# Attention and two feed-forward layers on one core: later chunks of the weights kept as 32-bit words until block 1, and a later place for block 2's attention

## The chip, the cores and the metric

The kernel runs on one core of a Trainium2 chip. The metric is device microseconds of a whole execution. Several executions were timed and their median counts; one more was recorded by the hardware profiler, and the trace comes from it. TensorE is the matrix engine, DVE the vector engine, ACT the scalar engine, POOL the general one, and SP issues every DMA of this kernel.

## The reference

The inputs q, k and v are float32 of 4 batches, 8 heads, 576 positions and 64 elements. The weights of the feed-forward layers are float64.

```
scores = q k^T / 8                       # per batch and head
keep the 32 largest of each row; softmax over these
x = attn v, heads side by side           # 2304 tokens x 512
h = relu(x w_in);  x = (h*h) w_out       # w_in 512x2048, w_out 2048x512
h = max(x w1, x w2, x w3);  out = h w_out2   # w1..w3 512x768, w_out2 768x512
```

## The kernel before

**Blocks.** The 2304 tokens are worked on in six blocks of 384 columns. The list `units` says which 128-row tiles of which batch belong to a block. Block 0 is three tiles of batch 0; block 1 is the rest of batch 0 and the first tile of batch 1; block 2 is the other three tiles of batch 1, and blocks 3 to 5 do the same for batches 2 and 3. For each block, `attend` runs four times (one pair of heads each), and then `moe` runs both feed-forward layers. Block 2 finds the keys and values of batch 1 prepared already, and loads queries only; the calls of block 3 load and prepare those of batch 2.

**Attention.** A job is one head of one tile, 24 jobs or more to a block. TensorE makes the scores (L525), ACT writes them to `s` (L446), DVE takes the 32 largest in four rounds of max8 and match_replace (L452, L454), ACT forms the exponentials (L312, L460), ACT and POOL split them into two f16 halves (L463, L309), SP transposes both by DMA (L468), TensorE multiplies by the values (L479), POOL divides and adds (L530 to L538), and TensorE transposes into the feed-forward operand `xt`, which ACT and DVE write as a high and a low part (L507, L509; L491, L493 for the 64 remaining rows). All four pairs of a block must be there before its first feed-forward matmul.

**Weights.** A weight is used as a pair: a rounded part and the remainder. Its source is float64, so it is converted once. There are 28 chunks of two halves, 16 for the first layer, 9 for w1 to w3 and 3 for w_out2. `half_chunk` converts a half: it loads 512 KB of raw float64 into one of three slots (L588), ACT makes a float from the high words (L589, recorded at L312) and takes the missing low bits from bytes (L592), DVE joins both into an exact 32-bit word in a buffer `ot` (L594, 3 buffers; the list `joined` keeps these operations), ACT rounds it (L597), POOL subtracts (L598, recorded at L309), and SP stores the 512 KB pair to DRAM (L599). The first 18 chunks (`EARLY`) are converted during block 0's attention, two halves to a job. The other ten are converted in block 0's feed-forward just ahead of their use, straight into one of seven `wt` buffers, and stored from there. Every later block loads pairs from DRAM to `wt` (L576).

**Order.** Nothing is left to run-time choice. `Plan` writes down one order for each engine at build time: a list scheduler takes, among what is ready on an engine, what can start first, by estimated times and with a small weight for priority. `fix_order` then holds each engine to it. Buffers of a tag are opened in the order of the program. `plan.after` adds a soft dependence: an operation may not start, in the plan's estimate, before the named one starts. It sets no semaphore. For the pairs of blocks 2 to 5 (`i >= NP * 3`) it names `joined[-9]`, the ninth last of the 56 joins, for everything that `attend` issues, the loads too; `moe` is free of it.

Of the kernel before, what the change touches and what calls it, by code (L numbers as in the profile page):

```python
# [10 lines left out]
F32 = mybir.dt.float32  # L11
F32R = mybir.dt.float32r
# [9 lines left out]
P = 128  # L22
# [227 lines left out]
def c_act(n, psum=True, ptr=0):  # L250
    return (55.0 if psum else 95.0) + 0.834 * n + 93.0 * ptr
# [6 lines left out]
def c_pool(n):  # L258
    return 100.0 + 2.18 * n
# [7 lines left out]
def kernel(ctx, tc, q, k, v, w_in, w_out, w1, w2, w3, w_out2, out):  # L267
    nc = tc.nc
# [3 lines left out]
    NP = H // 2  # L272
# [11 lines left out]
    dr = ctx.enter_context(tc.tile_pool(name="dr", bufs=1, space=DRAM))  # L284
    plan = Plan(nbufs, {"b"})

    def buf(tag, shape, dtype=F32):
        return Buf(plan, ppool if tag in ("a", "b") else spool, shape, dtype, tag)

    def keep(tile_):  # L290
        return Buf(plan, None, None, None, None, fixed=tile_)

    def act(prio, n, reads, writes, fn, psum=True, ptr=0):
        plan.op(ACT, c_act(n, psum, ptr), prio, reads, writes, fn)

    def dve(prio, n, reads, writes, fn, rate=1.0, slack=0.0):
        return plan.op(DVE, c_dve(n, rate), prio, reads, writes, fn, slack=slack)

    def gps(prio, n, reads, writes, fn):
        plan.op(POOL, c_pool(n), prio, reads, writes, fn)  # L300
# [4 lines left out]
    def dma(prio, nbytes, reads, writes, fn, ns=650.0):  # L305
        plan.op(SP, ns, prio, reads, writes, fn, lat=max(nbytes / DBW, 90.0))

    def sub(eng, out_ap, a, b):
        eng.tensor_tensor(out_ap, a, b, op=ALU.subtract)  # L309

    def prelu(out_ap, src, slope, **kw):
        return nc.scalar.activation(out_ap, src, AF.Prelu, alpha=slope, **kw)  # L312


    C_D, C_A, C_P, C_M = 1, 0, 0, 1
    A_S, A_X, A_E, A_V, M_, W_, MA, MP, MD = 0, 1, 2, 2, 4, -1, -1, 0, 0
# [25 lines left out]
    EARLY, PER = 18, 2  # L342
# [75 lines left out]
    def attend(i, unit, p):  # L418
# [18 lines left out]
        for j, h in jobs:  # L437
            for _ in range(min(PER if g == 0 else 0, len(ahead))):
                half_chunk(False, *ahead.pop(0))
# [104 lines left out]
    joined = []  # L544
# [8 lines left out]
    for fp in range(NF2):  # L553
        chunk_src.append(w_out2[fp * 256:(fp + 1) * 256, :].rearrange("(k p) f -> p k f", p=P))
    NCH = len(chunk_src)
    scratch = [[keep(dr.tile([P, 1024], F32, name=f"wsc{n}_{x}")) for x in range(2)] for n in range(NCH)]

    def weights(g, n):

        src = chunk_src[n]  # L560
        a, f = src.shape[1], src.shape[2]
        h = a // 2
        wts = [half_chunk(g > 0 or n < EARLY, n, x) for x in range(2)]

        def view(r, kk):
            return wts[kk // h][:, r].rearrange("p (a f) -> p a f", f=f // 2)[:, kk % h]
        return (lambda kk: wts[kk // h]), view

    def half_chunk(again, n, x):

        src = chunk_src[n]
        h, f = src.shape[1] // 2, src.shape[2]
        src = src[:, x * h:(x + 1) * h, :]
        wt, dst = buf("wt" if again or n >= EARLY else "cw", [P, 2, 512], F32R), scratch[n][x]
        if again:
            dma(W_, P * 4096, [dst], [wt], lambda: nc.sync.dma_start(  # L576
                wt[:].rearrange("p a b -> p (a b)").bitcast(F32), dst[:]))
            return wt
        raw = work[(2 * n + x) % len(work)]
        cv = buf("ot", [P, 512])  # L580

        def bits(t=U32):
            return spare[:].rearrange("p x a b -> p (x a b)")[:, 1024 * raw[1]:1024 * raw[1] + 1024].bitcast(t)

        def word(u):
            return bits().rearrange("p (n u) -> p n u", u=2)[:, :, u]

        dma(W_, P * 4096, [], [raw], lambda: nc.sync.dma_start(bits().rearrange("p (a f) -> p a f", f=f), src))  # L588
        act(C_M, 512, [raw], [cv], lambda: prelu(  # L589
            cv[:], word(1).bitcast(F32), -2.0 ** 32, scale=2.0 ** -112), psum=False)  # L590
        lw = buf("lw", [P, 512], U32)
        act(C_M, 512, [raw], [lw], lambda: nc.scalar.activation(  # L592
            lw[:], bits(U8).rearrange("p (n u) -> p n u", u=8)[:, :, 3], AF.Copy, scale=1.0 / 32.0, bias=-15.5 / 32.0), psum=False)
        joined.append(dve(C_D, 512, [cv, lw], [cv], lambda: nc.vector.scalar_tensor_tensor(  # L594
            cv[:].bitcast(U32), cv[:].bitcast(U32), 3, lw[:], op0=ALU.logical_shift_left, op1=ALU.bitwise_or),
            rate=1.7, slack=SL / 2))
        act(C_A, 512, [cv], [(wt, 0)], lambda: nc.scalar.copy(wt[:, 0], cv[:]), psum=False)  # L597
        gps(C_P, 512, [cv, (wt, 0)], [(wt, 1)], lambda: sub(nc.gpsimd, wt[:, 1], cv[:], wt[:, 0].bitcast(F32)))  # L598
        dma(W_, P * 4096, [wt], [dst], lambda: nc.sync.dma_start(  # L599
            dst[:], wt[:].rearrange("p a b -> p (a b)").bitcast(F32)))  # L600
        return wt

    def moe(g):
# [14 lines left out]
        def nextw():  # L618
            w = weights(g, cn[0])
            cn[0] += 1  # L620
            return w
# [94 lines left out]

    ahead = [(n, x) for n in range(EARLY) for x in range(2)]
    for i in range(NP * len(units)):
        plan.after = joined[-9] if i >= NP * 3 else None
        u = units[i // NP]  # L720
        attend(i, u, i % NP)
        if i % NP == NP - 1 and (i // NP == len(units) - 1 or units[i // NP + 1][3] != u[3]):
            plan.after = None
            moe(u[3])
# [66 lines left out]
```

## Time and profile before

| | |
|---|---|
| median of 3 runs | 1076.9 us (1076.82 to 1080.04) |
| profiled execution | 1079.8 us, span in the trace 1078.0 us |
| TensorE matmul busy | 984.3 us (91%) |
| TensorE weight load busy | 889.7 us (83%) |
| DVE busy | 818.7 us (76%) |
| ACT busy | 767.8 us (71%) |
| POOL busy | 625.3 us (58%) |
| mean granted TensorE clock | 0.958 |

Busy shares of the whole span hide the stages: attention and conversion run in the first part, and the last part has feed-forward layers alone. In the rows below, a `windows` row gives the stretch, and for each engine its busy time and, in brackets, its instructions; a timeline row gives start, duration, engine, line, operation, output and inputs, how many were merged, and in square brackets how long the engine sat idle before it and what released it. SPq is SP's queue, which issues DMAs in order and can wait.

### The profile page before, as it was taken

How to read it: one execution, taken by the hardware profiler on the slowest of the kernel's cores; microseconds unless marked ns; L12 is line 12 of the kernel's file. 1: busy time of each engine (PE TensorE's matmuls, PEld its weight loads, DVE VectorE, ACT ScalarE, POOL GpSimd, SP SyncE). 2: the span in 40 equal slices, each digit the busy share in tenths (PEclk: the TensorE clock that was granted, in tenths of full speed). 3: DMA queues.
4: the chain of work that ended last, by engine and by line, in shares of the span. 5: the costliest groups of instructions: out<-in, count | busy, mean ns of one | idle time of the engine just before them, and what ended most of it. 6: DMA issues, size and time to landing. Idle time of an engine off the chain costs nothing.

```text
span 1078.0 us, 18812 instructions
## 1 busy us (share of the span) xinstructions
PE 984.3 (91%) x6116; PEld 889.7 (83%) x6116; DVE 818.7 (76%) x1736; ACT 767.8 (71%) x1616; POOL 625.3 (58%) x887
## 2 busy tenths in 40 slices
PE   5556576999998999999999999999999999999998
PEld 3333343799897899998999998999998999989997
DVE  5999899899976999999999999999999601100020
ACT  6987788899887889976788868888876742123311
POOL 2666677787787577756467676767565641112210
PEclk9999755799999999999999999999999999999999
DMA  9999899999998999999999999999999986787774
GB/s 306 348 308 251 256 285 332 245 269 231 251 341 318 316 348 283 288 288 256 300 261 266 281 284 274 267 237 262 254 256 280 285 261 237 252 266 262 257 239 147
DMA packets 249697, 295.04 MB, mean 274 GB/s; under 512 B 178944, under 2 KB 182528, under 8 KB 249600
## 3 DMA queue, kind: packets, MB, share of 16 engines
q1 hardware_dynamic: 249600, 293.85, 95.1%
q8 instruction: 48, 0.79, 0.3%
q14 instruction: 49, 0.40, 0.1%
HBM read 217.25 MB, written 34.08 MB: 233 GB/s over the span
## 4 chain that ended last, share of the span: by engine, by line
PE 61%; DVE 13%; ACT 11%; POOL 7%; DMA 4%; issue 3%; SPq 0%; POOLq 0%; ACTq 0%; DVEq 0%
PE a L630 37%; PE b L630 13%; DVE mx L452 7%; DVE w L454 6%; PE b L525 5%; PE b L479 4%; DMA xt<-in_moe_w_in_dram 2%; POOL e L309 2%; ACT s L446 1%; ACT e L312 1%; POOL hl L309 1%; DMA xt<-in_moe_w_dram 1%; ACT lw L592 1%; ACT e L460 1%; ACT ot L312 1%
## 5 line engine op out<-in xcount | busy, mean ns | idle before, releaser
L452 DVE MAX8 mx<-w 128x8 f32<-128x576 f32 x432 | 311.1, 746 | 0.1
L309 POOL TENSOR_TENSOR e<-e,e 128x512 f16<-128x512 f32 (+1 forms) x288 | 211.9, 748 | 108.6 <-ACT e L463 91.3
L630 PE MATMUL a<-xt,wt 128*128 128x384 f32 x1296 | 239.3, 339 | 1.0 <-DVE xt L309 0.9
L630 PE MATMUL b<-xt,wt 128*128 128x384 f32 x1152 | 235.9, 346 | 3.5 <-DMA wt<-wsc 1.9
L630 PE MATMUL a<-hh,wt 128*128 128x384 f32 x768 | 228.8, 346 | 0.0
L630 PEld LDWEIGHTS a<-xt,wt 128*128 128x128 f32 x1296 | 224.1, 188 | 2.2 <-DVE xt L309 1.9
L454 DVE MATCH_REPLACE8 w<-mx,w 128x576 f32<-128x576 f32 x288 | 213.1, 742 | 0.0
L630 PEld LDWEIGHTS b<-xt,wt 128*128 128x128 f32 x1152 | 203.8, 192 | 5.8 <-DMA wt<-wsc 1.9
L525 PE MATMUL b<-kt,qt 128*128 128x288 f32 (+1 forms) x640 | 167.9, 395 | 36.2 <-DMA qt<-in_q_dram 17.8
L309 POOL TENSOR_TENSOR hl<-r,hh 128x384 fp32r<-128x384 f32 x96 | 97.3, 1014 | 126.5 <-ACT hh L656 119.2
L525 PEld LDWEIGHTS b<-kt,qt 128*128 128x128 f32 (+1 forms) x640 | 118.1, 218 | 62.5 <-ACT xs L482 16.4
L630 PEld LDWEIGHTS a<-hh,wt 128*128 128x128 f32 x768 | 142.7, 190 | 2.1 <-issue 1.1
L630 PE MATMUL a<-hl,wt 128*128 128x384 f32 x384 | 131.3, 342 | 4.1 <-POOL hl L309 3.8
L312 ACT ACTIVATE e<-s,mx 128x576 f32<-128x576 f32 x144 | 112.2, 779 | 27.7 <-POOL e L309 16.5
L479 PEld LDWEIGHTS <-et 128*128 128x128 f16 (+1 forms) x1440 | 84.1, 108 | 57.6 <-issue 35.4
L446 ACT ACTIVATE s<-b 128x288 f32<-128x288 f32 x288 | 108.0, 409 | 24.8 <-PE b L525 23.2
L479 PE MATMUL b<-vt,et 128*128 128x129 f16 (+3 forms) x1440 | 101.7, 223 | 25.2 <-DMA et<-e 16.8
L460 ACT ACTIVATE e<-e,nb 128x576 f32<-128x576 f32 x144 | 112.1, 779 | 6.8 <-POOL nb L456 4.8
L452 DVE MAX8 mx<-s 128x8 f32<-128x576 f32 x144 | 107.2, 746 | 10.3 <-ACT s L446 10.3
L454 DVE MATCH_REPLACE8 w<-mx,s 128x576 f32<-128x576 f32 x144 | 106.8, 742 | 0.0
L654 ACT ACTIVATE r<-b 128x384 f32<-128x384 f32 x96 | 47.1, 490 | 79.2 <-PE b L630 76.6
L463 ACT CAST e<-e 128x576 f16<-128x576 f32 x144 | 96.6, 672 | 1.6 <-DMA et<-e 1.3
(62 smaller groups left out, 1194.8 us busy)
## 6 DMA issues: line engine op xcount, KB each, us to landing
wt<-wsc SPq DMA_DIRECT2D x316, 512.0 KB, 4.8
wsc<-cw SPq DMA_DIRECT2D x36, 512.0 KB, 4.9
xt<-in_moe_w_out_dram SPq DMA_DIRECT2D x22, 512.0 KB, 6.3
wsc<-wt SPq DMA_DIRECT2D x20, 512.0 KB, 5.7
xt<-in_moe_w_dram SPq DMA_DIRECT2D x18, 512.0 KB, 5.9
xt<-in_moe_w_in_dram SPq DMA_DIRECT2D x16, 512.0 KB, 5.8
ks<-in_k_dram SPq DMA_DIRECT2D x12, 576.0 KB, 5.9
vst<-in_v_dram SPq DMA_DIRECT2D x16, 320.0 KB, 5.8
```

What stands on the lines that cost most here:

```text
L309: eng.tensor_tensor(out_ap, a, b, op=ALU.subtract)
L312: return nc.scalar.activation(out_ap, src, AF.Prelu, alpha=slope, **kw)
L446: act(A_S, HS, [ps], [(s, f)], lambda s=s, cs=cs, ps=ps: nc.scalar.activation(s[:, cs], ps[:, 0:HS], AF.Copy, scale=escale))
L452: dve(A_X, S, [src], [(mx, r)], lambda src=src, mx=mx, m8=m8: nc.vector.max(out=mx[:, m8], in_=src[:]))
L454: dve(A_X, S + 50, [src, (mx, r)], [w_], lambda src=src, mx=mx, m8=m8, w_=w_: nc.vector.match_replace(out=w_[:], in_to_replace=mx[:, m8], ...
L460: act(A_E, S, [e, nb], [e], lambda nb=nb, e=e: nc.scalar.activation(e[:], e[:], AF.Exp, bias=nb[:], scale=-1.0 / KEEP), psum=False, ptr=1)
L463: act(A_E, S, [e], [(e16, 0)], lambda e=e, e16=e16: nc.scalar.copy(e16[:, S:2 * S], e[:]), psum=False)
L479: nc.tensor.matmul(ps[0:m, 0:wv], et[:, mm_, c0:c1], vt[:, hh, vc, 0:wv], start=x == 0, stop=x == 8)
L525: nc.tensor.matmul(ps[:, 0:HS], a, c, start=m == 0, stop=m == len(seq) - 1)
L592: act(C_M, 512, [raw], [lw], lambda: nc.scalar.activation(lw[:], bits(U8).rearrange("p (n u) -> p n u", u=8)[:, :, 3], AF.Copy, scale=1.0 ...
L630: nc.tensor.matmul(o, x, y, start=first and i == 0 and m == 0, stop=last and i == n - 1 and m == 2)
L654: act(MA, N, [ps], [r], lambda r=r, ps=ps: nc.scalar.activation(r[:, 0:N], ps[:, 0:N], AF.Relu))
```

## The change

The ten chunks that are not converted early (20 halves) are stored by block 0 as joined 32-bit words, 256 KB a half, from `ot`. Block 0's own use of them stays as it was. Block 1 no longer loads pairs for these chunks: it loads the words into an `ot` buffer, rounds on ACT and subtracts on POOL into `wt`, and stores the pair of 512 KB to the place from which blocks 2 to 5 load it. The soft dependence of blocks 2 to 5's attention names the fifth last join in place of the ninth last.

```diff
+    words = [[keep(dr.tile([P, 512], F32, name=f"w32_{n}_{x}")) for x in range(2)] for n in range(NCH)]
...
-        wts = [half_chunk(g > 0 or n < EARLY, n, x) for x in range(2)]
+        wts = [split(n, x) if g == 1 and n >= EARLY else half_chunk(g > 0 or n < EARLY, n, x) for x in range(2)]
...
         act(C_A, 512, [cv], [(wt, 0)], lambda: nc.scalar.copy(wt[:, 0], cv[:]), psum=False)
         gps(C_P, 512, [cv, (wt, 0)], [(wt, 1)], lambda: sub(nc.gpsimd, wt[:, 1], cv[:], wt[:, 0].bitcast(F32)))
+        if n >= EARLY:
+            dma(W_, P * 2048, [cv], [words[n][x]], lambda: nc.sync.dma_start(words[n][x][:], cv[:]))
+            return wt
         dma(W_, P * 4096, [wt], [dst], lambda: nc.sync.dma_start(
             dst[:], wt[:].rearrange("p a b -> p (a b)").bitcast(F32)))
         return wt
 
+    def split(n, x):
+
+        wt, dst, cv = buf("wt", [P, 2, 512], F32R), scratch[n][x], buf("ot", [P, 512])
+        dma(W_, P * 2048, [words[n][x]], [cv], lambda: nc.sync.dma_start(cv[:], words[n][x][:]))
+        act(C_A, 512, [cv], [(wt, 0)], lambda: nc.scalar.copy(wt[:, 0], cv[:]), psum=False)
+        gps(C_P, 512, [cv, (wt, 0)], [(wt, 1)], lambda: sub(nc.gpsimd, wt[:, 1], cv[:], wt[:, 0].bitcast(F32)))
+        dma(W_, P * 4096, [wt], [dst], lambda: nc.sync.dma_start(
+            dst[:], wt[:].rearrange("p a b -> p (a b)").bitcast(F32)))
+        return wt
...
-        plan.after = joined[-9] if i >= NP * 3 else None
+        plan.after = joined[-5] if i >= NP * 3 else None
```

## Rows read from the trace of the kernel before

**Rows 1.** Windows by stage: us, busy (x) of PE, PEld, DVE, ACT, POOL; PEclk, DMA, GB/s

```profile
0.00:200.00 200.00, 122.34 (x437) 76.57 (x438) 178.89 (x362) 165.59 (x332) 126.20 (x164) 0.81 0.99 296
340.00:370.00 30.00, 23.49 (x108) 19.13 (x108) 29.66 (x61) 26.37 (x54) 19.59 (x20) 0.89 0.88 285
370.00:1078.00 708.00, 699.40 (x4617) 664.89 (x4615) 493.51 (x1067) 456.87 (x972) 370.11 (x548) 1.00 0.94 266
```

**Rows 2.** Windows, a stretch of 5 us at the end of block 0

```profile
345.00:350.00 5.00, 1.84 (x5) 1.16 (x6) 4.66 (x11) 4.81 (x11) 4.82 (x3) 0.59 0.46 147
```

**Rows 3.** Timeline of PE, 343 to 363 us

```profile
346.85 0.79 PE L630 MATMUL a<-wt,hh 128*128 128x512 f32 x1 [1.25 <-ACT wt L597]
349.33 0.79 PE L630 MATMUL a<-wt,hh 128*128 128x512 f32 x1 [1.69 <-POOL wt L309]
...
352.83 0.62 PE L630 MATMUL a<-wt,hh 128*128 128x512 f32 x2
...
361.79 1.50 PE L630 MATMUL b<-xt,wt 128*128 128x384 f32 x7 [1.46 <-DMA wt<-wsc]
```

**Rows 4.** Chain of waits, 300 to 520 us: start, us, what

```profile
344.57 3.04 POOL kt L309
...
355.07 6.67 DMA wt<-wsc
...
500.27 4.95 PE a L630 x21
```

**Rows 5.** Windows: block 0's conversions; block 1's use of the same chunks

```profile
286.00:344.00 58.00, 57.07 (x379) 52.62 (x377) 41.35 (x77) 48.07 (x103) 45.60 (x53) 1.00 1.01 339
445.00:507.00 62.00, 61.20 (x421) 57.98 (x420) 61.27 (x135) 46.24 (x100) 37.77 (x61) 1.00 1.01 280
```

**Rows 6.** Timeline of DVE, 318 to 356 us: joins (L594), block 2's first maximum

```profile
319.41 1.37 DVE L594 SCALAR_TENSOR_TENSOR ot<-ot,lw 128x512 uint32<-128x512 uint32 x1 [2.39 <-ACT lw L592]
...
336.67 0.68 DVE L594 SCALAR_TENSOR_TENSOR ot<-ot,lw 128x512 uint32<-128x512 uint32 x1
338.59 0.76 DVE L452 MAX8 mx<-s 128x8 f32<-128x576 f32 x1 [1.24 <-ACT s L446]
...
344.23 0.27 DVE L493 SCALAR_TENSOR_TENSOR xt<-b,us,xt 128x64 fp32r<-128x64 f32 x1
344.41 0.68 DVE L594 SCALAR_TENSOR_TENSOR ot<-ot,lw 128x512 uint32<-128x512 uint32 x1
...
353.50 1.67 DVE L594 SCALAR_TENSOR_TENSOR ot<-ot,lw 128x512 uint32<-128x512 uint32 x1
```

**Rows 7.** Timeline, end of block 2's attention and start of its feed-forward

```profile
489.40 0.75 DVE L452 MAX8 mx<-w 128x8 f32<-128x576 f32 x1
...
506.77 0.61 DVE L509 SCALAR_TENSOR_TENSOR xt<-b,us,xt 128x384 fp32r<-128x384 f32 x1
...
514.64 0.69 PE L630 MATMUL b<-xt,wt 128*128 128x384 f32 x3
```

**Rows 8.** DMA issues: what, KB each, median us to landing

```profile
out_dram<-ot SPq DMA_DIRECT2D x16, 256.0 KB, 5.1
...
xt<-in_moe_w_dram SPq DMA_DIRECT2D x18, 512.0 KB, 5.9
```

**Rows 9.** Groups by line: x count, busy us, mean ns, idle before

```profile
L312 ACT ACTIVATE ot<-xt 128x512 f32<-128x512 f32 x56 | 37.5, 670 | 12.8 <-POOL cw L309 9.8 <-DMA xt<-in_moe_w_in_dram 2.0 <-POOL wt L309 0.5
...
L309 POOL TENSOR_TENSOR wt<-ot,wt 128x512 fp32r<-128x512 f32 x20 | 27.3, 1369 | 7.3 <-ACT wt L597 4.5 <-DVE mx L452 2.3
...
L597 ACT CAST wt<-ot 128x512 fp32r<-128x512 f32 x20 | 12.4, 623 | 5.4 <-DVE ot L594 3.0 <-PE b L630 1.4 <-PE a L630 0.9
```

**Rows 10.** Timeline of SP and ACT: block 2's first query load and cast

```profile
323.25 0.57 SPq L354 DMA_DIRECT2D qs<-in_q_dram  x1
...
334.00 0.84 ACT L413 CAST qt<-qs 128x768 fp32r<-128x768 f32 x1
```

**Rows 11.** Tile of the query loads, 320 to 340 us

```profile
DMA to landing us min/median/max: 6.1/6.5/6.9
```

## The prediction

> **What bounds the kernel now.** I read the stages first, then the seam between blocks 0 and 1, then the end of block 2's attention, because these are the two places that the change touches on the path.
>
> TensorE is the bound once it has work. In the first 200 us it is idle for 77.7 us, with no feed-forward work before block 0's attention is done; from 370 us to the end it is idle for 8.6 of 708 us [rows 1]. So what counts is when feed-forward work starts and whether it stops. It stops once, in 340 to 370 us, where TensorE is idle for 6.5 us [rows 1]. There the last three chunks of block 0 are still being converted. Its matmuls wait at 346.85 us for a cast and at 349.33 us for a POOL subtraction, and the granted clock of 345 to 350 us is 0.59 on the mean, the lower level of 1.2 GHz for much of that time [rows 2, 3]. Nine matmuls of 512 columns run between 346.85 and 352.83 us; at the 0.236 us each that such a run takes elsewhere (4.95 us for 21) they need 2.1 us [rows 3, 4]. Of the 5.98 us between, 1.69 are the wait at 349.33 and so counted already; 5.98 - 1.69 - 2.1 leaves 2.2 us lost to the slow clock. All together the seam loses 6.5 + 2.2 = 8.7 us. The chain of waits names the holders: a 3.04 us key subtraction on POOL, which belongs to block 3's preparation and stands ahead of a weight subtraction, and then a 6.67 us wait for block 1's first weights, issued at 355.07 us [rows 4].
>
> The second limit lies behind it. Block 2's attention runs on a DVE that has 61.3 of 62 us busy [rows 5]. Its first maximum starts at 338.59 us, its last operand is written at 506.77 + 0.61 = 507.38 us, and block 2's feed-forward starts at 514.64 us [rows 6, 7]. The slack is 7.26 us. Whoever closes the seam by starting this attention later pays from those 7.26 us.
>
> **The change part by part.** The profiled execution took 1079.8 us, 2.9 above the median of the runs; I work out a difference from its trace and take it off the median, 1076.9.
>
> Block 0's stores. Twenty halves store 256 KB in place of 512 KB. A store then follows the join, not the POOL subtraction, so SP stands less long behind POOL, and a weight buffer is free when TensorE is done with it. This puts nothing on an engine. The `ot` buffer is instead held until the words have landed; the nearest row, a 256 KB store from such a buffer, has 5.1 us [rows 8]. Three `ot` and three raw slots each give one half per third of a round. The raw round is 5.9 us to land, 0.67 for the float pass, about as much for the byte pass, and about 1 us of queue: 8.2 / 3 = 2.75 us a half [rows 8, 9]. Before, the four joins from 319.41 to 336.67 us came 4.3 us apart, with block 2 and 3 preparation among them [rows 6]. These are my bounds for the spacing; I take 2.75, since the change moves just that preparation behind them.
>
> The later gate. It is an order in the written plan, not a semaphore: all of block 2's and later attention, its query loads included, comes after the fifth last join and not the ninth last. At the new spacing the fifth last falls at 319.41 + 4 x 2.75 = 330.4 us. From gate to first maximum, before: 3.84 us until the query load issues at 323.25, 6.5 to land, and a cast at 334.00 that leads to the maximum at 338.59, 4.6 us later [rows 6, 10, 11]; the rest of the 19.2 us was the cast standing in ACT's queue behind block 1's last pieces. Those are nearly done at the new gate, so I take a 2.3 us wait, between nothing and that 3.84: 2.3 + 6.5 + 4.6 = 13.4, a first maximum at 343.8 us, 5.2 late. Against that, four joins that DVE ran among this attention, from 344.41 to 353.50 us, 4.2 us together, now come ahead of it [rows 6]. Net: 1.0 us late. Bounds: 4.2 us early (no delay of the start, joins gone) and 13.1 late (old spacing and old 19.2 us).
>
> The seam. With block 3's preparation behind the gate, the last casts and subtractions stand free, and block 1's first weights no longer wait behind stores that wait for POOL. Block 1's last operand, at 344.23 us, is in time [rows 6]. TensorE can get back up to 8.7 us; I keep one spacing of 2.75 for the last chunk, which still comes just in time. So TensorE could reach block 2 about 6.0 us earlier. What is late next is block 2's attention.
>
> Block 1's second conversion. Twenty ACT casts of 0.62 us (12.5), twenty POOL subtractions of 1.37 us (27.4), and as many store issues on SP [rows 9]. ACT and POOL are busy 46.2 and 37.8 of the 62 us in which block 1 uses these chunks [rows 5]: 58.6 and 65.2 with the additions. ACT holds; POOL is 3.2 us over, so its queue is never empty. It hides behind seven weight buffers and behind block 3's attention, which isn't yet due; the job of block 2 that ends last isn't hidden. Its last maximum is at 489.40 us, and 18 us of ACT, POOL, SP and TensorE follow until 507.38 [rows 7]. I charge this chain one subtraction (1.37) and one cast (0.62) standing ahead of its own: 2.0 us. Bounds: 0, where the conversions are over by then, and 6.9, one subtraction ahead of each of five POOL steps. DMA bytes cancel: 20 x 256 KB less in block 0, as much less loaded and twice that stored in block 1.
>
> Sum. Attention: 1.0 + 2.0 = 3.0 us late, less the slack of 7.26: block 2's feed-forward starts 4.3 us earlier. TensorE's own side allows 6.0, so attention is last. All behind it is bound by TensorE, and the 4.3 stay: 1076.9 - 4.3 = 1072.6 us.
>
> **The rivals.**
>
> *Attention starts too late (slower).* The place is the gate. If joins keep the old 4.3 us and the way to the first maximum stays 19.2, it begins at 336.67 + 19.2 = 355.9 us: 13.1 + 2.0 - 7.26 = 7.8 us later, 1084.7. It decides from a first maximum at 338.59 + 4.2 + 7.26 - 2.0 = 348.0 us: beyond that the kernel is slower. For it: DVE is already idle for 16.7 of the 58 us from 286 to 344 us [rows 5], and the gate prolongs this. Against: the ACT queue that caused the old wait is shorter.
>
> *TensorE's side is last.* The attention gives up nothing (its start is covered by the joins, the conversions are over before the chain). Then the 6.0 decide: 1070.9, at most 8.7, 1068.2. For it: DMA moved 339 GB/s with 1.01 of its engines' time in 286 to 344 us [rows 5], so fewer bytes may bring raw chunks sooner. Against: the waits there name POOL and TensorE. The Trainium skill, DMA: Bandwidth & Descriptors, section Where 436 GB/s comes from, puts transfers between HBM and SBUF at about 358 GB/s. By that rule the block 0 stage stands near the ceiling, the removed 5.2 MB would be worth about 15 us of transfer there (an estimate from that page), and this rival would be the result; no row shows a whole stretch held by it.
>
> *Conversion paces block 1.* Its twenty halves have the 62 us and a lead of seven buffers (7/20 of that, 21.7 us): 83.7 us, and 6.0 more before the gain is gone, so beyond 4.5 us a half it is slower; at 4.8, 96 us, TensorE stands 6.3 longer than gained: 1083.2. For it: POOL is full and shared with the feed-forward remainders. Against: block 0 did better with five engine steps a half, and here there are two.
>
> *The gate moves nothing.* Had the plan block 2's attention after that join anyway, only the 1.46 us weight wait at 361.79 goes [rows 3]: 1075.4. Against: the query load of before stands directly behind the old gate.
>
> **How the numbers follow.** A measurement of this kernel can tell about 0.3%, 3.2 us. Chances: forecast 0.40, attention too late 0.22, TensorE's side 0.22, conversion pace 0.08, no move 0.08. The forecast's own range is 1070.9 to 1077.5 (a chain charge from 0 to 6.9, capped by TensorE's side), of which somewhat over half is below 1073.7. Faster by over 0.3%: 0.22 + 0.22 = 0.44. Within: 0.18 + 0.08 + 0.03 of the slower rivals = 0.29. Slower: 0.27. The range reaches from 1067 (TensorE's side, with a little from the new order) to 1084, which leaves out the end of the first rival.
>
> **What would show it.** Right: first maximum of block 2 between 340 and 348 us; TensorE without idle time in 340 to 352 and no clock under 1.0 there; block 1's feed-forward from about 350; block 2's last operand near 511 and its feed-forward right behind it, with TensorE waiting there for it. Wrong: a first maximum later than that, weight casts of block 1 that TensorE waits for, or idle time of TensorE over 3 us between 440 and 520 with a fall of its clock.

## The result and the profile after

The changed kernel took 1084.0 us (median of 5 runs, 1082.9 to 1085.0) against 1076.8 before: a ratio of 1.0055, interval 1.0033 to 1.0077. It is slower; the forecast was 1072.6. The profiled execution took 1085.0 us with a span of 1083.1.

The seam went as forecast. Windows of the changed kernel, with the columns of [rows 1, 2 and 5]:

```profile
340.00:370.00 30.00, 29.92 (x181) 26.91 (x180) 29.85 (x66) 25.09 (x55) 19.31 (x24) 1.00 1.03 345
345.00:350.00 5.00, 5.00 (x24) 3.79 (x22) 4.93 (x13) 2.70 (x6) 4.92 (x4) 1.00 1.00 343
370.00:1084.00 714.00, 695.32 (x4563) 657.42 (x4562) 491.12 (x1062) 462.07 (x984) 392.28 (x563) 1.00 0.94 265
445.00:507.00 62.00, 57.96 (x384) 53.98 (x383) 61.93 (x137) 49.98 (x105) 55.55 (x76) 0.97 1.02 283
```

TensorE's idle time in 340 to 370 us fell from 6.51 to 0.08 us [rows 1], and the clock there is 1.00. But from 445 to 507 us, where [rows 5] had 0.8 us of idle time at full clock, TensorE now idles for 4.0 us at 0.97, and POOL is busy for 55.6 us instead of 37.8. Split by stage, before:

```profile
440.00:480.00 40.00, 39.20 (x275) 37.83 (x274) 39.41 (x87) 32.55 (x72) 26.57 (x38) 1.00 1.01 293
480.00:515.00 35.00, 35.00 (x229) 31.67 (x228) 34.59 (x77) 24.55 (x52) 19.89 (x31) 1.00 1.01 272
515.00:560.00 45.00, 44.29 (x309) 42.52 (x309) 44.79 (x96) 35.48 (x79) 27.42 (x43) 1.00 1.02 272
```

and after:

```profile
440.00:480.00 40.00, 39.77 (x278) 38.39 (x277) 39.53 (x85) 32.31 (x70) 35.68 (x43) 1.00 1.01 290
480.00:515.00 35.00, 30.29 (x194) 25.52 (x193) 35.00 (x77) 30.19 (x65) 32.28 (x44) 0.95 1.02 291
515.00:560.00 45.00, 42.12 (x284) 38.98 (x283) 45.00 (x99) 34.20 (x75) 24.66 (x40) 1.00 1.14 311
```

The loss sits in 480 to 560 us: 4.71 + 2.88 us idle. DVE is full in both stretches (before, it had 0.4 and 0.2 us free there), and POOL nearly so in the first (32.3 of 35). The timeline of PE after, with the waits in brackets, names what TensorE waited for:

```profile
486.26 0.44 PE L644 MATMUL a<-xt,wt 128*128 128x384 f32 x1 [1.91 <-POOL wt L309]
...
495.68 0.49 PE L644 MATMUL a<-wt,hh 128*128 128x512 f32 x1 [0.47 <-ACT wt L611]
497.83 0.50 PE L644 MATMUL a<-wt,hh 128*128 128x512 f32 x1 [1.67 <-POOL wt L309]
...
511.61 0.50 PE L644 MATMUL a<-wt,hh 128*128 128x512 f32 x1 [0.67 <-POOL wt L309]
...
517.62 0.38 PE L380 MATMUL b<-sm,ones 128*128 128x1 f32 x2 [0.76 <-ACT vs L377]
```

The first four (4.7 us) are weights of block 1 from the second conversion; from 515 us on it is attention pieces that TensorE waits for (`vs`, `hl`, `xg`, 2.8 us). To add up over a run I take, for each 5 us window, TensorE's idle time plus (1 - granted clock) x its busy time, and call the sum the loss. In us, from one profiled execution of each:

| | 195-340 | 340-370 | 370-480 | 480-515 | 515-560 | 560-1070 | sum |
|---|---|---|---|---|---|---|---|
| before | 5.6 | 8.6 | 1.9 | 0.0 | 0.7 | 2.4 | 19.2 |
| after | 5.4 | 0.1 | 1.8 | 6.0 | 2.9 | 4.4 | 20.6 |

Of the 8.5 us that the seam gave, 8.2 went in 480 to 560 and 2.0 behind it. The rest of the 5.1 us between the spans lies, with 2.4, in the start (block 0's feed-forward began that much later in this execution, where the written order is still that of before) and 1.3 are not in this sum.

Landmarks, first activation of a block's feed-forward: block 1 at 365.62 before and 356.94 after; block 2 at 517.48 and 518.69; block 3 at 673.24 and 677.26. The end of block 2's attention and the start of its feed-forward, in the timelines of DVE and PE after, answer to [rows 7]:

```profile
506.18 0.60 DVE L509 SCALAR_TENSOR_TENSOR xt<-b,us,xt 128x384 fp32r<-128x384 f32 x1
...
514.60 0.69 PE L644 MATMUL b<-xt,wt 128*128 128x384 f32 x3
```

Attention was not late (506.78 against 507.38). TensorE still came at 514.60, where 4.3 us earlier than 514.64 was forecast, and left 7.8 us of slack: it was busy or waiting in block 1.

### The profile page after: what moved, and what is told of

Read it like the earlier page. It is cut to its first block, busy times and chain, and to the rows that moved or that the text cites. A ratio compares the mean times of both kernels' runs of the same rounds, so it can differ in the third digit from the quotient of the medians.

```text
span 1083.1 us, 18873 instructions
## 1 busy us (share of the span) xinstructions
PE 981.9 (91%) x6116; PEld 887.1 (82%) x6116; DVE 818.5 (76%) x1736; ACT 775.3 (72%) x1636; POOL 651.3 (60%) x907
## 4 chain that ended last, share of the span: by engine, by line
PE 62%; DVE 17%; ACT 9%; POOL 5%; issue 3%; DMA 3%; SPq 0%; POOLq 0%; ACTq 0%
PE a L644 38%; PE b L644 13%; DVE mx L452 8%; DVE w L454 7%; PE b L525 6%; PE b L479 4%; DMA xt<-in_moe_w_in_dram 2%; POOL hl L309 1%; ACT lw L593 1%; ACT s L446 1%; POOL e L309 1%; POOL cw L309 1%; ACT ot L312 1%; ACT e L312 1%; ACT e L460 1%
## 5 line engine op out<-in xcount | busy, mean ns | idle before, releaser
L525 PE MATMUL b<-kt,qt 128*128 128x288 f32 (+1 forms) x640 | 165.3, 393 | 38.6 <-DMA qt<-in_q_dram 20.6
L446 ACT ACTIVATE s<-b 128x288 f32<-128x288 f32 x288 | 108.2, 409 | 20.5 <-PE b L525 19.2
```

The costliest lines, as they stand in the source:

```text
L446: act(A_S, HS, [ps], [(s, f)], lambda s=s, cs=cs, ps=ps: nc.scalar.activation(s[:, cs], ps[:, 0:HS], AF.Copy, scale=escale))
L525: nc.tensor.matmul(ps[:, 0:HS], a, c, start=m == 0, stop=m == len(seq) - 1)
```

## The experiments

Ratios are to runs of the kernel before on the same chip, with the 95% interval. The median of the kernel before lay between 1076.8 and 1080.2 us from one set of runs to the next, so the ratios decide, and an expectation in us has to be read with that in mind. The theories: P, POOL's queue paces block 1's weights; O, the round through three `ot` buffers and SP's queue does; G, the later gate costs; W, the written order ties TensorE to attention, which DVE paces; and, once these had been tried, C, the second conversion stands in the way on ACT, POOL or SP whatever DVE does, D, POOL and DVE hold TensorE together, and Q, the order of the queues does, whatever the engines' speed.

**The gate alone, without words.**

```diff
-        plan.after = joined[-9] if i >= NP * 3 else None
+        plan.after = joined[-5] if i >= NP * 3 else None
```

> The kernel before with the later gate alone (fifth last join in place of the ninth last); pairs are stored by block 0 and loaded by block 1 as before. Theory P (block 1's second conversion fills POOL and paces the weights that TensorE waits for) and theory O (three ot buffers and SP's queue pace them) both put the whole loss on the conversion, so here the seam's gain stays at least in part: 1069 to 1075 us, block 1's first layer from 358 to 363 us, no TensorE wait on weights in 440 to 515. Theory G (the later gate is what costs): 1080 us or more, with block 2's last operand later than 510 us.

Measured: 1076.9 us, 0.9994 (0.9972 to 1.0016), between the two forecasts. Block 1's feed-forward began at 355.52 us, so most of the seam gain comes from the gate and needs no words: the loss there is 2.4 us instead of 8.6. The whole loss is 14.4 us, 4.8 below before, but the time is not measurably lower; the interval leaves room for up to 3 us. Of the 6.2 us that the seam gave, 3.2 went in 480 to 560 us, and no wait there is on a weight: the longest, 1.02 us, is on `s`. Windows of this kernel:

```profile
480.00:515.00 35.00, 31.97 (x209) 27.77 (x206) 34.58 (x75) 26.40 (x55) 19.13 (x31) 1.00 1.04 280
515.00:560.00 45.00, 44.14 (x311) 42.19 (x310) 45.00 (x98) 36.75 (x81) 29.50 (x46) 1.00 0.94 242
```

**Words with the old gate, and with a later one** (`joined[-9]` and `joined[-1]` in the changed kernel).

> The changed kernel with the old gate (ninth last join). Theories P and O: block 1 still converts twenty halves, so TensorE still waits there, and the seam gains less: 1080 to 1088 us. Theory G: 1070 to 1076 us.

> The changed kernel with the gate at the last join in place of the fifth last. With the gate at the ninth last it took 1096 us and at the fifth last 1084. Theory P: the later start takes attention out of POOL's queue in block 0 but not in block 1, and block 2's attention becomes late, so it is slower than the changed kernel: 1086 to 1095 us. Theory W: the time depends on the order and not on the amount of POOL work, and this can come out either way, 1076 to 1095.

Measured: 1096.1 us, 1.0169 (1.0145 to 1.0193), and 1082.4, 1.0026 (1.0009 to 1.0042). Words cost most at the early gate: there block 2's last `xt` activation came at 499.8 us, its feed-forward's first matmul only at 523.1, and 515 to 560 us lost 10.4 us. With words a later gate did not cost; the rival "attention starts too late" has the sign wrong. At the last join there is no run without words to compare with.

**Fewer words** (only the three chunks from 25 on, six halves, gate as changed).

```diff
+    WORDS = 25
...
-        if n >= EARLY:
+        if n >= WORDS:
```

> The changed kernel with words for the last three chunks alone (w_out2, 6 halves); the other 14 halves are stored as pairs by block 0 and loaded by block 1 as before. Theory P: POOL gets 8 us in block 1 in place of 26, so TensorE hardly waits there, and the seam keeps its gain: 1071 to 1077 us. Theory W: 1078 to 1084, since the last six halves are those for which TensorE waited longest.

Measured: 1079.8 us, 1.0008 (0.9995 to 1.0021). With none, six and twenty halves at this gate: 0.9994, 1.0008, 1.0055. By these intervals six halves cannot be told from none, and twenty can. Each amount also has a written order of its own. With six halves TensorE had no weight wait of 0.35 us or more in 480 to 560 us, and still lost 9.7 us there, at waits for attention pieces and with the clock at 0.89 from 515 to 560 us; its whole loss, 19.5 us, was close to the 19.2 of before.

**Without POOL's step; and without `ot`.** The first loads the word a second time in place of the low part (so the remainder is left out), the second converts within the weight buffer. Both change the written order.

```diff
-        gps(C_P, 512, [cv, (wt, 0)], [(wt, 1)], lambda: sub(nc.gpsimd, wt[:, 1], cv[:], wt[:, 0].bitcast(F32)))
+        dma(W_, P * 2048, [words[n][x]], [(wt, 1)], lambda: nc.sync.dma_start(wt[:, 1].bitcast(F32), words[n][x][:]))
```

> The changed kernel, but block 1 leaves out the POOL subtraction of its twenty halves: the low part of the pair is a second load of the word (256 KB more by DMA a half), so the low parts are not remainders. ACT's cast, the ot buffers and the stores stay. Theory P: POOL is 26 us lighter, TensorE does not wait for weights in 470 to 510, and the time falls by 6 to 10 us from the changed kernel, to 1073 to 1078. Theory O: the rounds of ot and SP stay as long or get longer, 1082 to 1088.

> The changed kernel, but block 1's words are loaded into the low part of the wt buffer and subtracted there in place, so ot is not used in block 1 and up to seven words can be on the way. The POOL subtractions stay. Theory P: 1081 to 1086 us, TensorE still waits for weights in 470 to 510. Theory O: 1073 to 1078 us.

Measured: 1107.5 us, 1.0268 (1.0242 to 1.0295), and 1089.7, 1.0111 (1.0088 to 1.0135). Both are outside both forecasts. The first has less POOL work and is 23 us slower: TensorE waits 11.0 us in two places for POOL's `xg`, an attention piece. The planner had other operations to place and wrote another order. Such a run tests that order, not the price of a step, so from here on every kernel keeps the changed kernel's order on PE, DVE, ACT and POOL (the control that of the kernel before).

**POOL's step halved, order kept.** A copy in place of the subtraction (remainder left out).

```diff
-        gps(C_P, 512, [cv, (wt, 0)], [(wt, 1)], lambda: sub(nc.gpsimd, wt[:, 1], cv[:], wt[:, 0].bitcast(F32)))
+        gps(C_P, 512, [cv, (wt, 0)], [(wt, 1)], lambda: nc.gpsimd.tensor_copy(wt[:, 1], wt[:, 0]))
```

> The changed kernel with every engine's order the same; only the twenty POOL subtractions of block 1 are replaced by a POOL copy of the rounded part, one input in place of two, so the remainder is left out. Theory P (POOL's time paces the weights): a copy takes perhaps half of 1.30 us, TensorE's waits on weights between 480 and 505 us shrink, block 2's first relu comes 4 to 8 us earlier than 518.7, and the time is 1076 to 1080 us. Theory W (the written order itself, in which the conversions stand behind attention pieces that come late on the chip, paces TensorE): no more than 2 us earlier, 1081 to 1085.

Measured: 1084.2 us, 1.0039 (1.0024 to 1.0055), which cannot be told from 1.0055. A step took 0.61 us in place of 1.30, yet in 480 to 515 us TensorE idled for 4.64 us in place of 4.71, mostly elsewhere. Windows, and the two longest waits in its PE timeline:

```profile
480.00:515.00 35.00, 30.36 (x202) 25.57 (x201) 35.00 (x78) 30.19 (x65) 26.53 (x43) 1.00 0.99 284
```

```profile
488.66 0.38 PE L380 MATMUL b<-sm,ones 128*128 128x1 f32 x2 [1.57 <-ACT vs L377]
...
507.29 0.50 PE L644 MATMUL a<-wt,hh 128*128 128x512 f32 x1 [1.49 <-POOL wt L612]
```

DVE is still at 35.00 of 35. POOL alone is not the pace.

**Six buffers; loads from ACT's queue; no loads.** The words land in six areas that block 0's conversions have left; the second also lets ACT issue the loads; the third leaves out nineteen loads and the subtraction.

```diff
-        dma(W_, P * 2048, [words[n][x]], [cv], lambda: nc.sync.dma_start(cv[:], words[n][x][:]))
+        dma(W_, P * 2048, [words[n][x]], [cv], lambda: nc.sync.dma_start(area(i), words[n][x][:]))
```

> The changed kernel with every engine's order kept, but block 1's twenty word halves land in six buffers that block 0's conversions have left, in place of the three ot buffers, so a word load waits for the subtraction six halves back and not for that three back. Theory O (a half's round through three ot buffers and SP's queue paces block 1's weights): TensorE's waits for wt in 480 to 515 us, 4.7 us in the changed kernel, fall below 2, its clock there stays above 0.98, and the time falls by 3 to 6 us, 1078 to 1081. Theory W (the written order ties TensorE to attention, which DVE paces): the weight waits shrink, but waits for vs, hl and xg take their place, idle time in 480 to 560 us stays at 6 us or more, and the time stays at 1083 to 1085.

> As the run with six buffers, and the twenty word loads are issued by ACT and not by SP, so they no longer stand behind SP's transposes (5.56 us for three at 481.02 us in the changed kernel) or behind a pair store that waits for POOL. Theory O in its SP form: weight waits of TensorE in 480 to 515 us fall below 1 us, also if six buffers alone did not do it; 1077 to 1080. Theory O in its buffer form: as with six buffers alone. Theory W: 1083 to 1085, with waits for attention in the place of those for weights.

> The changed kernel with the same order on PE, DVE, ACT and POOL, but nineteen of block 1's twenty word loads are left out: cast and second part are made from one half that stays resident, and POOL copies in place of subtracting (the weights of block 1's ten late chunks are thus not the right ones, and their low parts neither). What is left of the conversion is a cast and a short copy as soon as a weight buffer is free. Theory O: no weight wait of over 0.5 us in 480 to 515 us; 4.7 us of idle time and about 1.5 us of slow clock go, 1084.0 - 6.2 = 1077.8, between 1076 and 1080. Theory W: TensorE runs ahead to attention and waits there; idle time in 480 to 560 us stays at 5 us or more, 1082 to 1085.

Measured: 1082.6 us, 1.0037 (1.0022 to 1.0053); 1088.4, 1.0091 (1.0067 to 1.0114); 1083.1, 1.0040 (1.0024 to 1.0056). With six buffers the four weight waits are 1.91, 0.48, 1.67 and 0.65 us, those of the changed kernel within 0.02; with ACT's queue 1.80, 0.42, 1.69 and 0.65. Without loads they are 0.35, 0.77, 1.46 and 0.37, within 0.03 of those with POOL's copy alone. Theory O falls: neither buffers nor SP's queue nor the loads pace the weights. Theory W, a DVE pace, was left.

**DVE relieved, and the control.** From the second round on the score search looks at half the columns, in blocks 2 to 5; the same cut in the kernel before.

```diff
-                dve(A_X, S, [src], [(mx, r)], lambda src=src, mx=mx, m8=m8: nc.vector.max(out=mx[:, m8], in_=src[:]))
+                dve(A_X, S, [src], [(mx, r)], lambda src=src, mx=mx, m8=m8, c=cut(r): nc.vector.max(out=mx[:, m8], in_=src[:, 0:c]))
```

> The changed kernel, all orders kept, with less work for DVE in the attention of blocks 2 to 5: from the second round on the search for the 32 largest scores looks at 288 of 576 columns (so the threshold of those rows is found from half the scores). That takes about 5 x 0.37 = 1.9 us from each job's 5.3 us on DVE. Theory W (the written order ties TensorE to an attention that DVE paces, 35.00 of 35 and 45.00 of 45 us busy in 480 to 560): the waits for wt, vs, hl and xg in 480 to 560 us, 7.6 us with 1.3 of slow clock, fall below 2.5, and the time falls by 6 to 9 us, 1075 to 1078. Rival C (block 1's second conversion stands in the way on ACT, POOL or SP whatever DVE does): the weight waits of 4.7 us stay above 3.5, and the time stays at 1081 to 1084.

> The control: the kernel before, all orders kept, with the same cut of DVE's work in the attention of blocks 2 to 5 (half the columns from the second round on). Its TensorE loses only 0.7 us in 480 to 560 us and 8.6 at the seam, which DVE does not set, so both theories expect 1073 to 1077. Theory W: the changed kernel with the same cut ends within 2 us of it or ahead of it, as the seam is then a gain that nothing takes back. Rival C: the changed kernel with the cut ends 5 us or more behind it.

Measured: 1082.3 us, 1.0036 (1.0022 to 1.0050), and the control 1078.0, 0.9993 (0.9978 to 1.0009). DVE had 8 of 35 us free, and the weight waits did not move (4.6 us), as rival C had it. Windows and PE timeline of the changed kernel with DVE relieved:

```profile
480.00:515.00 35.00, 30.41 (x194) 25.71 (x194) 26.89 (x79) 30.06 (x64) 32.30 (x44) 0.95 1.00 292
```

```profile
486.45 0.44 PE L645 MATMUL a<-xt,wt 128*128 128x384 f32 x1 [1.89 <-POOL wt L309]
...
498.01 0.50 PE L645 MATMUL a<-wt,hh 128*128 128x512 f32 x1 [1.66 <-POOL wt L309]
```

Its POOL timeline shows why: a queue with hardly a gap. The subtraction that ends the wait at 486.45 is the first of the three in the last row. Its cast had ended at 483.89 us and TensorE stood from 484.56, but POOL came to it only at 485.12, behind attention pieces (`e`, `nb`, `vt`).

```profile
478.99 1.32 POOL L309 TENSOR_TENSOR wt<-ot,wt 128x512 fp32r<-128x512 f32 x1
480.24 1.72 POOL L309 TENSOR_TENSOR e<-e,e 128x64 f16<-128x64 f32 x3
482.05 0.29 POOL L457 TENSOR_SCALAR nb<-mx 128x1 f32<-128x1 f32 x1
482.42 1.43 POOL L309 TENSOR_TENSOR e<-e,e 128x512 f16<-128x512 f32 x2
483.81 1.36 POOL L309 TENSOR_TENSOR vt<-vs,vt 128x640 f16<-128x640 f32 x1
485.12 3.78 POOL L309 TENSOR_TENSOR wt<-ot,wt 128x512 fp32r<-128x512 f32 x3
```

Theory W falls as well, as one engine's pace. Where DVE is relieved POOL holds, and where POOL is relieved DVE has no gap. The changed kernel ended 4.3 us behind the control, between the two forecasts for that. Rival C in its POOL and SP forms does not hold alone either: with POOL's step halved and the loads gone, the run without loads was still at 1.0040. ACT's casts were left in every run.

**Both relieved.** The cut of DVE together with POOL's copy, and that without loads.

```diff
-                        out=w_[:], in_to_replace=mx[:, m8], in_values=src[:], imm_value=-3.0e38))
+                        out=w_[:, 0:c], in_to_replace=mx[:, m8], in_values=src[:, 0:c], imm_value=-3.0e38))
...
-        gps(C_P, 512, [cv, (wt, 0)], [(wt, 1)], lambda: sub(nc.gpsimd, wt[:, 1], cv[:], wt[:, 0].bitcast(F32)))
+        gps(C_P, 512, [cv, (wt, 0)], [(wt, 1)], lambda: nc.gpsimd.tensor_copy(wt[:, 1], wt[:, 0]))
```

> The changed kernel, all orders kept, with DVE relieved (half the columns from the second round of the score search on, blocks 2 to 5) and POOL relieved (block 1's twenty subtractions are copies, so the low parts of those weights are left out) at once. Theory D (DVE and POOL both hold TensorE in 480 to 560 us, each when the other is relieved): idle time and slow clock there, 9.1 us with DVE relieved alone and 8.3 with POOL alone, fall below 4, and the time falls to 1076 to 1079, level with the control's 1078.0. Theory Q (the order of the queues: TensorE's places, ACT's casts among score copies that wait for TensorE, whatever the engines' speed): the loss stays above 7 us and the time at 1081 to 1084.

> As the run with DVE and POOL relieved, and nineteen of the twenty word loads are left out too (cast and copy read one half that stays resident; those weights are not the right ones). Only the cast, the copy and the pair stores of the second conversion are left. Theory D: 1075 to 1079 and a loss below 4 us in 480 to 560 us. Theory Q: 1081 to 1084, the loss above 7.

Measured: 1079.2 us, 0.9999 (0.9984 to 1.0014), and 1079.1, 0.9997 (0.9979 to 1.0015). Level with before and with the control. As ratios: nothing relieved 1.0055, POOL 1.0039, DVE 1.0036, both 0.9999. Either one alone cannot be told from nothing relieved; the second on top of the first is clear of noise (1.0039 or 1.0036 to 0.9999, intervals of about 0.0015 to each side). The two together give back 0.0056, more than the 0.0016 + 0.0019 of each alone, but that they do more than their sum is not shown. Without the loads nothing more is gained. In time theory D holds. In the trace it holds in part: the loss in 480 to 560 us is 6.2 us with both relieved and 7.5 without loads, where below 4 was expected; these are single executions, and the loss does not follow the time in every run. Windows with both relieved:

```profile
480.00:515.00 35.00, 32.41 (x215) 27.75 (x214) 28.56 (x85) 31.84 (x69) 28.44 (x48) 1.00 1.06 308
515.00:560.00 45.00, 41.44 (x279) 38.48 (x279) 31.90 (x99) 34.50 (x75) 26.04 (x41) 1.00 1.10 312
```

The remaining waits are `vs` (1.57 and 1.42 us) and pieces of 0.4 to 0.9, one of them a weight, with no engine but TensorE over 32 of 35 us on the mean. With what is lost behind 560 us they are about what the seam gave. The wait of 1.57 us is there with POOL's copy too, and 1.56 us long in both runs without loads, with DVE relieved or not. The ACT timeline with both relieved shows what stands before it:

```profile
484.75 0.62 ACT L612 CAST wt<-ot 128x512 fp32r<-128x512 f32 x1
...
485.94 0.61 ACT L612 CAST wt<-ot 128x512 fp32r<-128x512 f32 x1
...
488.38 0.62 ACT L612 CAST wt<-ot 128x512 fp32r<-128x512 f32 x1
488.88 0.75 ACT L377 ACTIVATE vs<-vst 128x640 f32<-128x640 f32 x1
```

ACT has no gap from 483.49 us on, and three casts of the second conversion, 1.85 us together, run ahead of `vs`. That these casts, a part of the conversion that no run took away, hold TensorE there is read from this trace alone: a run without them is missing, and so is the gate alone with DVE relieved. How much of the rest belongs to the order of the queues (theory Q) is open. No version ran measurably faster than the kernel before.

## Why the prediction was wrong

**Gate: right in kind, too dear.** Five joins up to 332.09 us came 2.2 to 2.8 us apart, where 2.75 was forecast. Timelines of DVE, SP and ACT after, against [rows 6 and 10], with the fifth last join first:

```profile
326.96 0.90 DVE L595 SCALAR_TENSOR_TENSOR ot<-ot,lw 128x512 uint32<-128x512 uint32 x1 [1.67 <-ACT ot L312]
...
339.02 1.42 DVE L452 MAX8 mx<-s 128x8 f32<-128x576 f32 x2 [1.21 <-ACT s L446]
```

```profile
328.26 0.44 SPq L354 DMA_DIRECT2D qs<-in_q_dram  x1
```

```profile
334.49 0.84 ACT L413 CAST qt<-qs 128x768 fp32r<-128x768 f32 x1 [0.22 <-DMA qs<-in_q_dram]
```

The fifth last join fell at 326.96 and not at 330.4, the load followed 1.3 us later and not 2.3, and the first maximum came at 339.02 instead of 343.8: 0.4 us late, not 5.2. Block 2's last operand came 0.6 us early, where the sum had 3.0 us late. In the changed kernel attention was not the last thing.

**Seam: right, and larger.** TensorE got 8.5 us back there, where 6.0 was forecast and 8.7 was the most. Most of it needed no fewer bytes: the gate alone reached block 1 at 355.52 us and gave 6.2. With words, 200 to 340 us moved 264 GB/s where it had been 280, and TensorE's loss from 195 to 340 us stayed (5.4 against 5.6 us). The Trainium skill, DMA: Bandwidth & Descriptors, section Where 436 GB/s comes from, has the HBM side, at about 358 GB/s, bind transfers between HBM and SBUF. The mean of 280 GB/s before lay below that figure, and the 15 us that the prediction estimated from that figure did not come.

**The step that failed: "Block 1's second conversion. ... It hides behind seven weight buffers and behind block 3's attention, which isn't yet due".** It was charged 2.0 us, on block 2's last attention chain, with bounds of 0 and 6.9. Its price, words against no words at the same gate, is 1.0055 / 0.9994 = 1.0061, 6.6 us (by the two intervals, some 3 to 10), and with it goes the other order that the planner wrote for it. In the changed kernel it falls first on TensorE's weights: 4.7 us of waits and the fall of the clock. The durations were about right (20 casts of 0.63 and 20 subtractions of 1.30 us). The sum "POOL is 3.2 us over" was not: POOL was busy for 55.6 of the 62 us and not 65.2, as about sixteen of the twenty subtractions fell in them. The larger error was what was made of that sum: a queue that is never empty was taken to hide work, and a lead of seven buffers was taken for granted, but the trace shows subtractions that end just as TensorE's wait for them ends. The rival "conversion paces block 1" asked for over 4.5 us a half to make the kernel slower; the halves came 3.86 us apart (casts from 435.38 to 508.70 us) and it was slower nonetheless. The wait at 486 us is set by where a subtraction stands in POOL's queue, as the POOL timeline with DVE relieved shows for the same wait, and not by the mean pace.

**"All behind it is bound by TensorE, and the 4.3 stay": wrong.** Of the 8.5 us nothing stayed, and with the gate alone, without any conversion, a seam 6.2 us better gave a time that is not measurably lower. DVE has 61.3 of 62 us in [rows 5], and the forecast read that as a limit on block 2's attention alone. That DVE bounds all attention pieces between 480 and 560 us, so that a TensorE that comes earlier waits there, fits both kernels (DVE 45.00 of 45 us from 515 to 560 us) and is argued, not shown: with DVE relieved alone the loss there stayed at 9.0 us, and only with POOL relieved as well did the time fall.

The signs named as "wrong" ahead of the run came: TensorE waits for block 1's weights, though only 0.47 us of it for a cast and the rest for subtractions, and it idles for over 3 us between 440 and 520 with a fall of its clock.

## What to carry to other kernels

In a stage that had one engine at its limit, work added to other engines did not hide behind buffers: look at the queue in which it stands, and at what waits behind it, before charging nothing. A gain at one stage can go in a later one that has another engine full; sum idle time and slow clock by stage to see where it goes, as landmarks also move with reordered work. Test the price of a step with all orders held fixed, and when two engines are full, relieve both at once: here each alone showed nothing clear of noise.

## What the runs showed of the hardware

- TensorE waited 1.91 and 1.67 us within 12 us, and in the 5 us of the second wait the clock fell. Windows of the changed kernel:

```profile
490.00:495.00 5.00, 5.00 (x46) 4.51 (x46) 5.00 (x14) 4.63 (x9) 4.39 (x7) 1.00 1.01 380
495.00:500.00 5.00, 2.86 (x13) 2.00 (x11) 5.00 (x12) 3.63 (x9) 5.00 (x8) 0.83 0.88 163
500.00:505.00 5.00, 5.00 (x31) 4.25 (x30) 5.00 (x12) 2.80 (x6) 4.20 (x9) 0.83 1.06 317
```

  A mean of 0.83 over 495 to 505 us means the lower level, 1.2 GHz, for about a third of it. In the run with POOL's copy, whose longest waits were 1.57 and 1.49 us, 19 us apart, it stayed at 1.00. With both relieved and no loads, it was 0.66 from 485 to 490 us, right behind a single wait of 1.56 us. So the length of a wait alone does not tell whether the clock falls.
- POOL took 1.30 us for a subtraction of two 128 x 512 float32 operands and 0.61 for a copy of one.
- With the word loads issued from ACT's queue, SP's transposes of 445 to 480 us held their queue for 3.58 us each (median of 6) instead of 2.61 in the changed kernel and 2.40 with the same loads on SP, and ACT waited 5.4 us for them. That kernel was 0.5% slower than with the loads on SP.
